# Step 8's rows by transposing transfer, a GpSimd drain put in order, and step 3's hidden values in two halves of columns

## Chip, core and metric

The kernel runs on one core of a Trainium2 chip: TensorE (PE), VectorE (DVE), ScalarE (ACT), GpSimd (POOL), SyncE (SP), which issues most transfers, and 16 DMA engines. The metric is the time of one execution in device microseconds, as the median of some runs. Profiles come from one execution that is profiled.

## What is computed

A feature-map attention over 8 batches, 8 heads and 576 positions of width 64, and behind it a mixture of 8 experts, of which each of the 4608 tokens takes one:

```python
x = attention(q, k, v, omega).reshape(4608, 512)
xn = x / (norm(x) + 1e-6); en = expert_emb / (norm(expert_emb) + 1e-6)
logits = xn @ en.T / tau
expert_idx = argmax(logits, axis=1)
gate_w = probs[arange(N), expert_idx]          # softmax of the logits
for e in range(8):
    mask = expert_idx == e
    h = maximum(x[mask] @ w1[e], 0.0)          # 512 -> 1024
    out[mask] = gate_w[mask, None] * (h @ w2[e])   # 1024 -> 512
```

All of it is float32. The kernel reaches that with float32r products: each operand is split into a rounded high part and what is left of it, and three products (high by high, high by low, low by high) are summed.

## The kernel before

**Two stages.** The first computes the attention in 36 tiles of 128 tokens and scatters each token's row from GpSimd into a table `xs` sorted by expert (L503). Two steps of the expert stage (steps 0 and 1, `first_steps`) are fitted into its last iterations; their outputs are the first two scatters to `y` (`store`, L270). The second stage is the loop over steps `t` = 2 to 37, in an order written out by hand for all engines (`manual_schedule`). A step is 128 rows of one expert.

**What a step does.** PE makes `pa` (rows by `w1`: two banks of 512 columns, 12 matmuls each) and `nu` (hidden values by `w2`: 24 matmuls), 48 in all. From step 6 on, the `nu` of a step belongs to the step two earlier, and step 5 has none. Rows and hidden values must be turned round (tokens to columns) before they can be used as PE's stationary operand. There are two ways:

- `turned` (L223): four PE transposes into a PSUM bank (`pt`), then ACT writes the high part (L227) and DVE the low part (L228).
- The transposing transfers: `apart16` (L924) splits 512 float32 columns into two planes of 16-bit words, one by DVE (L922, `moved`), one by ACT (L926). `turned16` (L929) has SP issue one transposing transfer for each plane (`t_<step>_0`, `t_<step>_1`, L933). When they have landed, `rejoin` (L941) puts the words together in `wd`: the hidden columns by DVE (L922), the row columns by ACT (L947). Then come `x_rounded` (L958, `xh`) and `x_left` (L962, `xl`) for the rows, and `summed` for the hidden values (L966 on ACT, `hh`, and L968 on DVE, `hl`).

The planes of step `t` take the hidden values of step `t` (1024 columns) and, where `far` holds, the rows of step `t + 2` (512 more). `XPE` = 9 is the first step whose rows go that way; rows of the steps before are turned on PE in the step ahead of their use. In steps 8 and 9 (`t in (XPE - 1, XPE)`) `xl` is made before the second `rejoin` of the hidden columns, in later steps behind it.

**What sets the order.** Each engine runs its own list in the order of the loop. SP issues, in this order within a step: a quarter of `w1`, a quarter of `w2`, the row block of step `t + 3` (`xload`, L158) and the two transposing transfers of step `t`. The planes have one buffer, so ACT's first `apart16` of a step waits until the transfers of the step before have read them. Row blocks live in a ring of six: the load of step 8's rows goes into the buffer of step 2's, and waits for step 2's scatter to `y`, which step 5 issues (`ended`, L1036) behind the scaling on DVE (L247). Every load of rows also waits for the one before it.

**Step 3's hidden values** are rejoined in step 4 (`early`): two rejoins of 1024 columns on DVE, `hh` of 1024 columns on ACT, `hl` of 1024 columns on DVE. Step 4's `nu` matmuls need both.

**The drain.** At `t == NPRE` (2) GpSimd gets a `drain` (L1020). Nothing ties it to its place. Other drains stand at every ninth step (L1051) and near the end (L1141).

Of the kernel before, what the change touches and what calls it, by code (L numbers as in the profile page):

```python
# [11 lines left out]
F32 = mybir.dt.float32  # L12
# [4 lines left out]
AF = mybir.ActivationFunctionType  # L17
ALU = mybir.AluOpType
# [6 lines left out]
E, F = 8, 1024  # L25
# [18 lines left out]
NSTAT = 38  # L44
WARM = 26
NSTEP = 64
XPE = 9
SHIFT = 5
BIGID = 1048576.0
EPS = 1e-6 * M  # L50
# [5 lines left out]
def attention_moe(ctx: ExitStack, tc: tile.TileContext, qT, kT, v1, omT, emb, tau, w1q, w2q, xs, out):  # L56
    nc = tc.nc
# [36 lines left out]
    first = const.tile([P, 1], F32, name="first")  # L94
# [8 lines left out]
    order = mybir.DependencyInfo(mybir.DependencyClass.NoSync, mybir.DependencyReason.DATA)  # L103
    put, got, outs, last_x, junks, early = [], [], [], [], [], []
# [173 lines left out]
    with ExitStack() as c1:  # L278
# [367 lines left out]
        mid, after, then, ends = {}, {}, {}, {}  # L646
# [207 lines left out]
    def sums(t, name, n):  # L854

        return [p2.tile([P, n], F32R, name=f"{name}{z}{t}", tag=f"{name}{z}", bufs=2) for z in "hl"]
# [6 lines left out]
    def halves(t, name, n):  # L863

        return placed.pop((name, t)) if (name, t) in placed else sums(t, name, n)
# [12 lines left out]
    def words(t):  # L878
        return p2.tile([P, F + DM], F32, name=f"wd{t}", tag="wd", bufs=1)
# [21 lines left out]
    xg, xt, hid, raws, po = {}, {}, {}, {}, {}  # L901
# [18 lines left out]
    def moved(to, src):  # L920

        nc.vector.tensor_reduce(to, src.unsqueeze(2), axis=AX.X, op=ALU.max)  # L922
# [14 lines left out]
    with tc.manual_schedule(engines={ET.PE, ET.Activation, ET.DVE, ET.Pool, ET.SP}):  # L937
        xt[NPRE] = pre_x[0]
        turn, ends = {}, NSTAT - 1

        def rejoin(u, wd, lo, hi, k):  # L941

            to, src = halved(wd)[:, lo:hi, k], turn[u][k][:, lo // P : hi // P].rearrange("p c r -> p (c r)")
            if lo < F:
                moved(to, src)
            else:
                nc.scalar.activation(to, src, AF.Copy)  # L947

        def joined(u):
            wd, n = words(u), turn[u][0].shape[1] * P  # L950
            assert n == F
            for k in range(2):
                rejoin(u, wd, 0, F, k)
            return wd, n
# [9 lines left out]
        def summed(u, wd):  # L964
            hid[u] = hh, hl = halves(u, "h", F)
            nc.scalar.activation(hh, wd[:, 0:F], AF.Relu)  # L966
            yield
            nc.vector.scalar_tensor_tensor(hl, wd[:, 0:F], 0.0, hh.bitcast(F32), op0=ALU.max, op1=ALU.subtract)  # L968
            yield
# [47 lines left out]
        for t in range(NPRE, NSTAT):  # L1017
            u = t - 1 if t < SHIFT else t - 2
            if t == NPRE:
                nc.gpsimd.drain()  # L1020
            far = XPE <= t + 2 < NSTAT
            near = t in (NPRE, ends)
            if t > NPRE + 1:
# [4 lines left out]
                weights("w2", t)  # L1028
            late = (t - 1) in turn
            early = late and (t < SHIFT or t == ends)  # L1030
            if early:
                sm = summed(t - 1, joined(t - 1)[0])
                next(sm)
                if t < ends:
                    next(sm)
            def ended():  # L1036

                for v in list(po):
                    scaled(po.pop(v), xg[v], gates[v])
                    store(v, xg[v])  # L1040
# [23 lines left out]
            computed("w1", t, products(pa[0], xt[t], "w1", par, low, 0, True, True))  # L1064
            if t == NPRE or NPRE + 1 < t < XPE - 1:
                xt[t + 1] = x_turned(t + 1, xg[t + 1])
            if near:
                h = words(t)
# [19 lines left out]
            if late and not early:  # L1088
                if wn[1] > F:
                    x_rounded(t - 1, wn[0])  # L1090
                    if t in (XPE - 1, XPE):
                        x_left(t - 1, wn[0])
# [6 lines left out]
            if late and not early:  # L1099
                sm = summed(t - 1, wn[0])  # L1100
                next(sm)
                if wn[1] > F and t not in (XPE - 1, XPE):
                    x_left(t - 1, wn[0])
# [48 lines left out]
    with tc.If(tot > NSTAT):  # L1152
        split("w1", ends)
        split("w2", ends)
        with tc.For_i(NSTAT, tot, 1) as i:
# [5 lines left out]
            h = hidden("x", x_turned("x", xgl), par)  # L1161
# [64 lines left out]
```

## Time and profile before

| | |
|---|---|
| median of 3 runs | 643.84 us (641.42 to 644.36) |
| profiled execution | 638.44 us, its span 636.9 us |
| PE, DVE, ACT, POOL busy | 620.7, 488.7, 414.3, 316.9 us |
| second stage on PE | from 232.4 us to the end |
| a step in its steady part | 10.88 us, 48 matmuls |

The page counts an engine as busy from an instruction's start to its end; matmuls overlap, and their starts are more exact than their ends. Times in the timeline are microseconds from the span's start. A bracket behind a row gives the idle time of the engine ahead of it, and who ended it. SPq is SP's queue of transfers: a row there is the issue, not the transfer itself. A row of windows gives the stretch, its length, then the busy time of PE, PEld, DVE, ACT and POOL with their instructions, TensorE's granted clock as a share of 2.4 GHz, the DMA engines' busy share and GB/s. In the chain of waits each piece is the work that the next one waited for.

### The profile page before, as it was taken

To read this page: it belongs to the slowest core of one execution; us is meant where nothing else is said; L and a number is where in the kernel's file an instruction comes from. 1 tells how busy PE (TensorE), PEld (TensorE's weight loads), DVE (VectorE), ACT (ScalarE), POOL (GpSimd) and SP (SyncE) were. 2 spreads that over 40 slices of the span, in tenths; PEclk is the share of its full clock that TensorE was granted. 3 is DMA by queue.
4 is the path that set the end of the run, shared out by engine and by line. 5 is a ranking of instruction groups with operands and counts; after the bars stand their busy time and mean duration, and the time that the engine had idled before them with its cause. 6 is when DMAs were issued, how large, how long until landed. Compare 5 with 4: busy or idle time off the path is not lost.

```text
span 636.9 us, 18610 instructions
## 1 busy us (share of the span) xinstructions
PE 620.7 (97%) x6339; PEld 531.2 (83%) x6340; DVE 488.7 (77%) x950; ACT 414.3 (65%) x1074; POOL 316.9 (50%) x404
## 2 busy tenths in 40 slices
PE   8999999999988999999999999999999999999996
PEld 7899999988877787788878888888888888888885
DVE  4799899899888736796788778788777778788652
ACT  6899899899977317654656565556565656565630
POOL 2014333337987434456365646464645555464623
PEclk9999999999999999999999999999999999999999
DMA  7547667678842278787988888888879897979741
GB/s 258 183 153 217 205 205 226 198 238 284 273 178 94 111 263 244 225 206 223 211 234 197 245 216 236 201 225 215 239 179 244 199 220 210 224 225 211 209 117 45
DMA packets 142362, 131.89 MB, mean 207 GB/s; under 512 B 106742, under 2 KB 106870, under 8 KB 142272
## 3 DMA queue, kind: packets, MB, share of 16 engines
q1 hardware_dynamic: 135808, 110.04, 65.4%
q0 software_dynamic: 6320, 20.38, 8.2%
q8 instruction: 57, 0.93, 0.6%
q10 hardware_dynamic: 144, 0.26, 0.2%
q14 instruction: 33, 0.27, 0.1%
HBM read 83.78 MB, written 21.97 MB: 166 GB/s over the span
## 4 chain that ended last, share of the span: by engine, by line
PE 72%; DVE 14%; ACT 6%; DMA 5%; issue 3%; POOL 0%; POOLq 0%; SPq 0%; DVEq 0%; ACTq 0%
PE pa L240 25%; PE nu L240 24%; PE pjk L328 5%; PE nub L424 4%; PE kva L354 4%; PE pjq L328 3%; DMA t<-pl 3%; DVE wd L922 3%; ACT ftk L339 2%; PE nub L400 2%; DVE nmq L332 2%; PE fs_o L240 2%; DVE pl L922 2%; PE fs_a L240 2%; ACT ftq L339 1%
## 5 line engine op out<-in xcount | busy, mean ns | idle before, releaser
L240 PE MATMUL nu<-w2h,hl 128*128 (+1 forms) x288 | 112.2, 390 | 0.5 <-DVE hl L968 0.5
L240 PE MATMUL nu<-w2h,hh 128*128 (+1 forms) x288 | 112.4, 390 | 0.0
L240 PE MATMUL nu<-w2l,hh 128*128 (+1 forms) x288 | 112.1, 389 | 0.0
L240 PE MATMUL pa<-w1h,xh 128*128 (+1 forms) x280 | 109.6, 391 | 0.1
L240 PE MATMUL pa<-w1h,xl 128*128 (+1 forms) x280 | 109.3, 390 | 0.3 <-DVE xl L962 0.3
L240 PE MATMUL pa<-w1l,xh 128*128 (+1 forms) x280 | 109.0, 389 | 0.0
L926 ACT ACTIVATE pl<-pa 128x512 uint16<-128x512 uint16 x68 | 39.9, 591 | 82.8 <-DMA t<-pl 59.7
L922 DVE TENSOR_REDUCE wd<-t 128x1024 uint16<-128x1024 uint16 x68 | 89.9, 1324 | 1.8 <-DMA t<-pl 1.8
L339 ACT ACTIVATE ftk<-pjk,nmk 128x128 f32<-128x128 f32 x288 | 85.4, 435 | 4.8 <-DVE nmk L332 4.6
L206 POOL TENSOR_TENSOR w1l<-raww,w1h 128x1024 f32 x33 | 80.2, 2431 | 10.1 <-DVE w1h L205 9.2
L339 ACT ACTIVATE ftq<-pjq,nmq 128x128 f32<-128x128 f32 x288 | 80.1, 433 | 7.6 <-DVE nmq L332 7.4
L922 DVE TENSOR_REDUCE pl<-pa 128x512 uint16<-128x512 uint16 x68 | 46.5, 686 | 46.2 <-ACT pl L926 45.7
L206 POOL TENSOR_TENSOR w2l<-raww,w2h 128x1024 f32 x33 | 79.5, 2408 | 3.8 <-DVE w2h L205 3.8
L328 PE MATMUL pjq<-om,qt 64*128 64x128 f32 x576 | 75.9, 283 | 1.5 <-ACT ftk L339 0.7
L966 ACT ACTIVATE hh<-wd 128x1024 fp32r<-128x1024 f32 x34 | 36.1, 1061 | 63.3 <-DVE wd L922 57.4
L328 PE MATMUL pjk<-om,kt 64*128 64x128 f32 x576 | 75.7, 283 | 0.3 <-DVE om L609 0.3
L328 PEld LDWEIGHTS pjk<-om,kt 64*128 64x128 f32 x576 | 64.4, 188 | 2.8 <-DVE om L609 0.5
L328 PEld LDWEIGHTS pjq<-om,qt 64*128 64x128 f32 x576 | 64.0, 188 | 2.3 <-ACT ftq L339 1.1
L240 PEld LDWEIGHTS nu<-w2h,hl 128*128 128x128 f32 x288 | 54.1, 188 | 12.1 <-DVE hl L968 0.9
L270 POOL DMA_INDIRECT y<-xgp x20 | 22.3, 1115 | 83.6 <-DVE xgp L247 75.0
L240 PEld LDWEIGHTS nu<-w2h,hh 128*128 128x128 f32 x288 | 54.0, 188 | 11.4 <-issue 0.2
L240 PEld LDWEIGHTS nu<-w2l,hh 128*128 128x128 f32 x288 | 54.1, 188 | 11.2
(311 smaller groups left out, 1258.9 us busy)
## 6 DMA issues: line engine op xcount, KB each, us to landing
raww<-w1q SPq DMA_DIRECT2D x38, 512.0 KB
raww<-w2q SPq DMA_DIRECT2D x38, 512.0 KB
qt<-qT SPq DMA_DIRECT2D x36, 256.0 KB
kt<-kT SPq DMA_DIRECT2D x35, 256.0 KB
xgp<-xs SPq DMA_DIRECT2D x20, 260.5 KB
xg<-xs SPq DMA_DIRECT2D x18, 260.5 KB
rf<-w1q SPq DMA_DIRECT2D x4, 512.0 KB
rf<-w2q SPq DMA_DIRECT2D x4, 512.0 KB
```

Of the source, the lines that this page charges most:

```text
L206: il = nc.gpsimd.tensor_tensor(at(l, dp), raw, at(h, dp).bitcast(F32), op=ALU.subtract)
L240: done.append(nc.tensor.matmul(dst, x[:, c * P : (c + 1) * P], ws.rearrange("p o f -> p (o f)"), start=(begin and i == 0 and k == 0), stop ...
L270: w = nc.gpsimd.indirect_dma_start(out=out, out_offset=bass.IndirectOffsetOnAxis(ap=xg[:, PAY - 1 : PAY].bitcast(I32), axis=0), in_=xg[:, ...
L328: nc.tensor.matmul(st["pj" + w, i, a][:, c, :], st[w, i][r, c, :], om[r, :], start=True, stop=True)
L332: nc.vector.tensor_reduce(nm, st["pj" + which, i, a], axis=AX.X, op=ALU.max, negate=True)
L339: nc.scalar.activation(ft[:, h, :], pj[:, h, :], AF.Exp, bias=nm[:, h : h + 1])
L354: nc.tensor.matmul(acc[c : c + 64, h, :], ft[:, h, c : c + 64], vt[:, 2 * h + a, :], start=begin and h == 0, stop=u == 4 + 4 * b and h == 3,)
L400: nc.tensor.transpose(nu[z][:, j * 64 : j * 64 + 64], st["fq", i, j // 4][r, j % 4, :], ident[r, r])
L424: nc.tensor.matmul(pn[a][z * 64 : z * 64 + 64, h, :], st["qp", i, z][:, 4 * a + h, :], kvs[sb, int(b)][:, h, a * HW : (a + 1) * HW], start ...
L922: nc.vector.tensor_reduce(to, src.unsqueeze(2), axis=AX.X, op=ALU.max)
L926: nc.scalar.activation(planes[1][:, o : o + 512], halved(src)[:, :, 1], AF.Copy)
L966: nc.scalar.activation(hh, wd[:, 0:F], AF.Relu)
```

## The change

Three edits. The first is one constant: `XPE` falls from 9 to 8. So step 8's rows ride along with step 6's hidden values (planes and transfers of 12 blocks of 128 columns and not 8), the four PE transposes of step 7 with their ACT and DVE work go, `rejoin`, `x_rounded` and `x_left` of rows come into step 7, and the steps in which `xl` is made early are 7 and 8 and no longer 8 and 9. The second ties the drain by an ordering without a wait to the last scatter to `y` so far. The profile of before has this drain at 2.4 us, ahead of the attention; the built program of after has it right behind the scatters of steps 0 and 1, ahead of step 0's split of `w2` on GpSimd. Nothing else on GpSimd changes its place. The third makes step 3's hidden values in two halves of columns: both rejoins and `hh` of one half, then of the other, then the two halves of `hl`.

```diff
-XPE = 9
+XPE = 8
...
             if t == NPRE:
-                nc.gpsimd.drain()
+                tc.add_manual_dep(nc.gpsimd.drain().ins, outs[-1].ins.name, order, reason="behind the first scatters")
...
-            if early:
+            if early and t < ends:
+                wd, hs = words(t - 1), halves(t - 1, "h", F)
+                hid[t - 1] = hs
+                parts = [slice(a * 512, (a + 1) * 512) for a in range(2)]
+                for c in parts:
+                    for k in range(2):
+                        rejoin(t - 1, wd, c.start, c.stop, k)
+                    nc.scalar.activation(hs[0][:, c], wd[:, c], AF.Relu)
+                for c in parts:
+                    nc.vector.scalar_tensor_tensor(hs[1][:, c], wd[:, c], 0.0, hs[0][:, c].bitcast(F32), op0=ALU.max, op1=ALU.subtract)
+            elif early:
                 sm = summed(t - 1, joined(t - 1)[0])
                 next(sm)
-                if t < ends:
-                    next(sm)
```

DVE in step 4, before: `wd` are the rejoined words, `t_3_0` and `t_3_1` the two transposed planes of step 3.

```order
L228 TENSOR_TENSOR xl_5616<-pt_5617,xh_5615 128x512
L922 TENSOR_REDUCE wd_5652<-t_3_0_5595 128x1024
L922 TENSOR_REDUCE wd_5652<-t_3_1_5597 128x1024
L968 SCALAR_TENSOR_TENSOR hl_5656<-wd_5652,hh_5655 128x1024
L145 TENSOR_LOAD tabi
```

The same place now:

```order
L228 TENSOR_TENSOR xl_5616<-pt_5617,xh_5615 128x512
L922 TENSOR_REDUCE wd_5652<-t_3_0_5595 128x512
L922 TENSOR_REDUCE wd_5652<-t_3_1_5597 128x512
L922 TENSOR_REDUCE wd_5652<-t_3_0_5595 128x512
L922 TENSOR_REDUCE wd_5652<-t_3_1_5597 128x512
L1040 SCALAR_TENSOR_TENSOR hl_5654<-wd_5652,hh_5653 128x512 x2
```

The rejoins come by halves of columns, each half with both planes, and `hl` has two instructions.

DVE in step 6, before: `pl_0` is DVE's plane, `t_5_0` and `t_5_1` the transposed planes of step 5.

```order
L922 TENSOR_REDUCE pl_0_5931<-pa_0_5933 128x512
L922 TENSOR_REDUCE wd_5970<-t_5_0_5899 128x1024
L922 TENSOR_REDUCE pl_0_5931<-pa_1_5934 128x512
L922 TENSOR_REDUCE wd_5970<-t_5_1_5901 128x1024
L968 SCALAR_TENSOR_TENSOR hl_5981<-wd_5970,hh_5980 128x1024
```

The same place now, where `xgp_103` holds the rows of step 8:

```order
L922 TENSOR_REDUCE pl_0_5935<-pa_0_5937 128x512
L922 TENSOR_REDUCE pl_0_5935<-xgp_103 128x512
L922 TENSOR_REDUCE wd_5976<-t_5_0_5903 128x1024
L922 TENSOR_REDUCE pl_0_5935<-pa_1_5938 128x512
L922 TENSOR_REDUCE wd_5976<-t_5_1_5905 128x1024
L968 SCALAR_TENSOR_TENSOR hl_5987<-wd_5976,hh_5986 128x1024
```

Step 8's rows have come in second place, ahead of the rejoin of step 5 and of the plane's second half, on which the transposing transfers of step 6 depend; ACT has the like for its plane.

ACT in step 7, before: `pt` is the bank of the PE transposes, `xg_5402` the rows of step 9, `pl_1` ACT's plane.

```order
L227 ACTIVATE xh_6052<-pt_6054 128x512
L926 ACTIVATE pl_1_6037<-pa_0_6038 128x512
L926 ACTIVATE pl_1_6037<-xg_5402 128x512
L926 ACTIVATE pl_1_6037<-pa_1_6039 128x512
L966 ACTIVATE hh_6087<-wd_6077 128x1024
```

The same place now:

```order
L926 ACTIVATE pl_1_6043<-pa_0_6044 128x512
L926 ACTIVATE pl_1_6043<-xg_5402 128x512
L947 ACTIVATE wd_6074<-t_6_0_5981 128x512
L947 ACTIVATE wd_6074<-t_6_1_5983 128x512
L926 ACTIVATE pl_1_6043<-pa_1_6045 128x512
L958 ACTIVATE xh_6085<-wd_6074 128x512
L966 ACTIVATE hh_6090<-wd_6074 128x1024
```

Step 8's `xh` has moved from the start of the step's row to its end, behind the planes and two rejoins that read step 6's transposed planes.

## Rows read from the trace of the kernel before

**Rows 1.** Windows, one a step (4, 7, 8, 11, 12): length, then busy by engine.
```profile
251.34:263.72 12.38, 11.87 (x53) 9.30 (x53) 9.08 (x11) 8.83 (x16) 6.11 (x3) 1.00 0.87 252
...
281.01:292.39 11.38, 11.38 (x54) 9.40 (x53) 8.73 (x15) 6.59 (x15) 6.16 (x4) 1.00 0.84 220
292.39:303.27 10.88, 10.88 (x50) 9.01 (x49) 7.58 (x12) 4.33 (x9) 5.95 (x3) 1.00 0.91 237
...
325.02:336.45 11.43, 11.18 (x49) 8.94 (x48) 8.62 (x13) 4.61 (x10) 6.03 (x4) 1.00 0.82 227
336.45:347.55 11.10, 11.10 (x50) 8.94 (x49) 8.76 (x12) 7.97 (x13) 5.95 (x3) 1.00 0.84 201
```

**Rows 2.** Timeline of PE at the end of step 4's first part.
```profile
257.70 0.40 PE L240 MATMUL nu<-w2l,hh 128*128 128x512 f32 x1
258.60 0.50 PE L240 MATMUL nu<-w2h,hl 128*128 128x512 f32 x1 [0.51 <-DVE hl L968]
```

**Rows 3.** The chain of waits, in order of time: start, length, what; steps 6 to 11.
```profile
269.83 0.61 ACT pl L926
...
281.45 5.22 DMA t<-pl
...
324.46 1.39 DVE xl L962
...
325.89 5.28 PE pa L240 x22
```

**Rows 4.** Timeline of DVE in step 4.
```profile
253.57 2.62 DVE L922 TENSOR_REDUCE wd<-t 128x1024 uint16<-128x1024 uint16 x2 [1.78 <-DMA t<-pl]
257.32 1.23 DVE L968 SCALAR_TENSOR_TENSOR hl<-wd,hh 128x1024 fp32r<-128x1024 f32 x1 [1.13 <-ACT hh L966]
```

**Rows 5.** Timeline of PE in step 7: the transposes.
```profile
283.73 0.60 PE L226 MATMUL pt<-ident,xgp 128*128 128x128 f32 x4
```

**Rows 6.** Timeline of SP's queue, steps 6 and 7.
```profile
276.70 0.33 SPq L158 DMA_DIRECT2D xgp<-xs  x1
...
279.71 0.33 SPq L158 DMA_DIRECT2D xg<-xs  x1
280.10 4.57 SPq L933 DMA_TRANSPOSE t<-pl  x2
...
292.08 0.33 SPq L158 DMA_DIRECT2D xg<-xs  x1
292.52 3.52 SPq L933 DMA_TRANSPOSE t<-pl  x2
```

**Rows 7.** What SP's queue waited for, 275 to 281 us: total, times, longest.
```profile
SPq L158 <- DMA y<-xgp: 2.6, 1, 2.6
SPq L158 <- DMA xgp<-xs: 0.9, 1, 0.9
```

**Rows 8.** Timeline of DVE, steps 6, 7 and 9.
```profile
278.91 0.67 DVE L922 TENSOR_REDUCE pl<-pa 128x512 uint16<-128x512 uint16 x1
...
289.74 0.66 DVE L922 TENSOR_REDUCE pl<-pa 128x512 uint16<-128x512 uint16 x1
...
313.12 0.76 DVE L962 TENSOR_TENSOR xl<-wd,xh 128x512 fp32r<-128x512 f32 x1
```

**Rows 9.** Timeline of ACT at the start of steps 7 and 8.
```profile
286.69 0.60 ACT L926 ACTIVATE pl<-pa 128x512 uint16<-128x512 uint16 x1 [1.14 <-DMA t<-pl]
...
298.49 0.60 ACT L926 ACTIVATE pl<-pa 128x512 uint16<-128x512 uint16 x1 [5.16 <-DMA t<-pl]
```

**Rows 10.** The drains by line: duration least, median, most (ns), first and last start.
```profile
L1020 POOLq DRAIN  x1: 406/406/406, 2.4 to 2.4; - x1
...
L1051 POOLq DRAIN  x3: 5648/5670/8961, 320.4 to 513.4; - x3
```

**Rows 11.** Timeline of POOL, steps 2 and 10.
```profile
243.01 4.77 POOL L203 TENSOR_TENSOR w2l<-raww,w2h 128x1024 fp32r<-128x1024 f32 x2 [7.08 <-ACT w2h L201]
...
322.88 2.40 POOL L206 TENSOR_TENSOR w2l<-raww,w2h 128x1024 f32 x1
```

## The prediction

> **What bounds the kernel now.** I read the windows step by step first. PE works without a gap in nearly all steps of the second stage: a step with 48 matmuls takes 10.88 us, so 0.227 us a matmul, and the granted clock stands at 1.00 of 2.4 GHz. Only where a step is longer can an edit gain anything [rows 1]. Step 4 has a wait for `hl`: the matmul that reads it starts 0.90 us behind the one before it, 0.67 more than the pitch [rows 2]. Step 7 is 0.50 longer than step 8, and the four transposes are what it has more [rows 1, 5]. Steps 11 and 12 are longer by 0.55 and 0.22. All other steps from 8 on take 10.88. So PE could win 0.67 + 0.50 + 0.55 + 0.22 = 1.94 us at most, 0.3% of the span.
>
> Then I read the chain of waits. From step 4 to step 6 it lies on PE. At 269.83 it leaves PE by the eviction of step 5's last bank and comes back only at 325.89, by `xl` of step 11 [rows 3]. Between these it runs in a loop: the transposing transfers land, ACT may write its plane, DVE evicts and rejoins, SP issues the next transfers. PE's wait in step 11 is this loop being late. So a gain on PE in steps 4 or 7 counts at the end only if the loop becomes earlier as well, and whatever makes the loop later counts in full. The rest of the working is about that loop.
>
> **Third edit, halves.** DVE's two rejoins run from 253.57 to 256.19; `hl` starts at 257.32 behind 1.13 of waiting for ACT [rows 4]. In halves the four rejoins take the same time, ACT's first `hh` fits under the last two, and half of `hl` (1.23 / 2) is ready at about 256.19 + 0.65 = 256.85, the rest one `hh` of half the columns and 0.6 later, at 257.5. PE wants the first half at 257.70 + 0.23 = 257.93 [rows 2] and the second 12 matmuls later. So the wait goes: -0.67, which moves PE in step 5 and with it the head of the loop. Next in line is `xl` of step 5, whose chain on DVE moves along.
>
> **Second edit, drain.** GpSimd is idle for 7.08 us ahead of 243.01, so from 235.93 on [rows 11], and the drain would start there. The drains in the trace last 0.41 to 8.96 us [rows 10], so this one ends between 236.3 and 244.9, and the split of `w2` behind it is late by 0 to 1.9. I take 0: two of the three drains of L1051 last 5.7, which is within the idle time. Below zero there is nothing, since PE waits for no work of GpSimd in these steps. What hides it is that idle time; its price without cover is a rival below.
>
> **First edit, what goes.** Four transposes on PE, 0.50 in step 7. ACT's and DVE's `turned` work of step 7 lies ahead of ACT's wait for the transfers of step 6, which ends at 286.69 [rows 9], and so frees nothing on the loop.
>
> **First edit, what comes.** In step 6 DVE and ACT must split the rows of step 8 in the middle of their planes. These rows are not there yet. Their load is issued at 276.70, held for 2.6 by step 2's scatter; the load behind it, at 279.71, waited for it to land [rows 6, 7]. So the rows land at about 279.65, 2.95 behind the issue. DVE is free for them at about 278.91 - 1.20 (the pitch of the rejoin ahead of that row) = 277.71 [rows 8]. It waits 1.94, works 0.60, and its second eviction moves from 278.91 to 281.45. With PE's 0.67 in hand at the head it is 280.8 and ends at 281.45; the transfers of step 6 are issued at 281.5 and not at 280.10, 1.4 later. ACT's split of the rows (0.6) goes on beside this.
>
> The transfers have 12 blocks now and not 8. From issue to ACT's release they took 6.59 with 8 blocks in step 6 (280.10 to 286.69) and 5.97 with 12 in step 7 (292.52 to 298.49) [rows 6, 9]. The lower bound is 5.97; the upper is 6.59 and half of the 4.57 that their issue took, 8.9. I take 6.6, nearest to both rows with a length, so ACT is released at 288.1, between 287.5 and 290.4, and not at 286.69.
>
> Step 7 then goes: release, 3.05 to DVE's second eviction (286.69 to 289.74), 0.66 for it [rows 8, 9]: the transfers of step 7 could be issued from 291.8 on. In the trace that was possible from 290.4 on, but SP stood until 292.08 in front of the load of step 10's rows, which waits for step 4's scatter, and issued them at 292.52 [rows 6]. So the loop has 1.7 of slack here, if that scatter is not late. It will be late by something: its scaling on DVE lies behind the rejoins of step 6, which have moved by 1.9. I take half, 0.9: the loop leaves step 7 by 0.9 later, with 0 and 1.9 as bounds.
>
> PE meanwhile: without waits step 8 begins at 292.39 - 0.67 - 0.50 = 291.22 and wants its `xl` two matmuls later, at 291.67. This `xl` comes 288.1 + 3.71 + 0.75 = 292.55, so PE waits 0.9. The hidden values of step 5 come 1.9 later too, at about 285; PE wants them at 286.3, so they are covered by 1.2.
>
> In step 9 `xl` (of step 10) moves behind one more rejoin, 1.3: from 313.12 to 314.4, done at 315.2, and 316.1 with the loop's 0.9 [rows 8]. Step 10 began at 303.27 + 10.88 = 314.15 and wants it at 314.6. So step 10 begins 1.5 later than before. After that PE is behind the loop: `xl` of step 11 at 325.85 + 0.9 = 326.75 is wanted at 325.47 + 1.5 = 326.97, and the waits of steps 11 and 12, 0.77, are gone.
>
> **Sum.** +1.5 - 0.77 = +0.73. On the profiled execution's 638.44 that is 639.2. The median of the three runs stands 5.4 above that execution, and I add the same 0.7 to it: 644.6. About 0.5%, 3.2 us, is what a measurement of this kernel can tell from no change, so the forecast is no difference.
>
> **Rivals.**
>
> The loop keeps up. If step 4's scatter lands no later than before, the loop leaves step 7 as it did: step 10 is then 0.6 late, 0.77 goes, -0.2 in all. If the loop's head carries its 0.67 through as well, it is -0.8, and with all waits gone -1.9. For it speaks the slack of 1.7, against it that DVE is later by 1.9 in step 6. About 643.4, from 641.9 to 643.7.
>
> GpSimd blocks DVE. `xl` of step 8 was computed out of PSUM; it will now read two operands in SBUF. Such an `xl` took 1.39 on the chain at 324.46, while GpSimd split `w2` from 322.88 to 325.28, and 0.76 at 313.12 [rows 3, 8, 11]. In step 7 GpSimd's two splits move by up to 1.9, to about where `xl` stands. If they meet, `xl`, the rejoin behind it and the rest of the loop are later by 0.6: 645.2. The Trainium skill has a rule on this (SBUF — State Buffer, Who interferes with whom): a DVE instruction with two SBUF inputs and a GpSimd instruction that reads SBUF exclude each other for a whole instruction. By that rule the trace agrees, with the 1.39 beside a GpSimd split.
>
> Slower: step 8's rows land late. They are the one new thing on which both ACT and DVE stand in step 6. The load waits for a scatter (2.6) and then takes 2.95 [rows 7]; each microsecond that either takes more moves the rejoins, the transfers of step 6 and, from 1.2 on, the hidden values for PE's step 7. From 2.5 on, so if the rows land behind 281.5 on this clock, the kernel is slower by over 0.5%; for 3 more it gives 644.6 + 3 = 647.6. Against it: the place of this load on SP's queue, and what stands ahead of it, have not changed.
>
> The drain holds GpSimd for 8.96 or more. The split of `w2` is then 1.9 late, with it the next weights and rows on SP's queue and, at worst, the transfers of step 3 by as much. `hl`'s first half comes at 258.75, and PE waits 0.8 where it waited 0.67. So edit three brings nothing and the loop starts 0.8 later than forecast: 645.4.
>
> The change does what it says, as the order of instructions shows; that the halves don't take PE's wait away is in the last rival.
>
> **Chances.** Forecast 0.46, loop keeps up 0.29, GpSimd blocks DVE 0.12, rows late 0.06, drain 0.05, anything else 0.02. Only late rows and part of the rest pass 0.5%: slower 0.05, faster 0.02, same 0.93. The range reaches from all PE waits gone (643.84 - 1.9 = 641.9) to the upper bound of the transfers of step 6, 2.3 more than taken (644.6 + 2.2 = 646.8).
>
> **What would show it.** In the profile after: step 4 at about 11.7 and no wait of PE for `hl`; a wait of DVE and ACT of 1 to 2 us for step 8's rows in step 6; ACT's release in step 7 near 288; PE waits for `xl` at the start of steps 8 and 10, and none in 11 and 12; a drain at about 236 that ends ahead of 243. I am wrong if steps 8 to 10 stay at 10.88 (the loop keeps up), if PE waits for hidden values in step 7 (rows late), or if the step 3 transfers are issued later than before (drain).

## The result and the profile after

The changed kernel takes 647.28 us (median of 22 runs), the kernel before 642.80 on the same chip (22 runs): a ratio of 1.0062, interval 1.0047 to 1.0078. That is 4.5 us more, just past the 0.5% that the prediction named as what can be told from no change; the forecast was +0.7. The runs of after also spread more, from 642.97 to 651.87, against 640.66 to 645.87: fourteen stand between 646.1 and 651.9, the other eight at or under 645.2.

The profiled execution of after is 647.85 (span 646.3) and stands 9.4 above the one of before (638.44). Not all of that is the change. The second stage begins at 236.44 on PE and not at 232.41, 4.0 later, but the execution of before that was profiled is faster than all 22 runs timed beside after. Whether the change makes the first stage longer is taken up with the experiments. From the start of the second stage to the start of step 14, behind which both kernels go at 10.88 a step, before takes 126.02 and after 131.33: +5.3. The windows of after (length, busy by engine, granted clock, DMA) for steps 2 with 3, 4, 7, 8, 9, 10 and 12 answer to [rows 1]:

```profile
236.44:258.14 21.70, 18.75 (x90) 14.88 (x88) 12.83 (x11) 13.25 (x21) 9.69 (x6) 1.00 0.82 278
258.14:271.30 13.16, 13.16 (x52) 10.59 (x53) 10.51 (x17) 8.73 (x18) 4.79 (x2) 0.87 0.77 232
...
288.61:299.49 10.88, 10.88 (x50) 9.01 (x48) 9.62 (x17) 7.32 (x16) 4.59 (x4) 1.00 0.90 252
299.49:312.17 12.68, 11.17 (x50) 8.93 (x48) 11.33 (x13) 5.07 (x9) 7.08 (x4) 1.00 0.69 187
312.17:323.72 11.55, 11.18 (x50) 8.94 (x49) 10.19 (x12) 7.20 (x12) 6.30 (x4) 1.00 0.78 211
323.72:334.78 11.06, 11.06 (x49) 8.93 (x48) 9.19 (x16) 7.76 (x18) 5.96 (x3) 1.00 0.85 218
...
345.66:356.89 11.23, 11.18 (x50) 8.94 (x48) 9.22 (x13) 8.32 (x14) 5.96 (x3) 1.00 0.84 213
```

Steps 2 and 3 took 18.93 before, so +2.77; step 4 +0.78; step 7 is 0.50 shorter, the four transposes; step 8 +1.80; step 9 +0.67; step 10 +0.18. Steps 11 to 13 together give 0.4 back. Two thirds of the loss stand in steps 2 to 4, where the forecast had a gain. The waits of PE in the second stage name what it waits for (total, times, longest):

```profile
PE pa L240 <- DVE w1l L203: 2.6, 1, 2.6
PE pa L240 <- DVE xl L962: 1.9, 2, 1.5
```

The first of them was no wait at all before. What stands behind it is the drain. By line (duration least, median, most in ns, first and last start), to be read against [rows 10]:

```profile
L1020 POOLq DRAIN  x1: 9688/9688/9688, 238.0 to 238.0; - x1
```

Such a row begins while GpSimd still works on what was queued ahead. Here that is a scatter until 239.92, so some 7.7 us are the drain's own, until 247.7; the last packets of the scatters end at 245.44 in the transfer records. The other three drains last 5.4 to 5.7 now, with two splits (4.8) inside, which leaves 0.6 to 0.8. GpSimd gets to its splits at 247.84, which is 11.40 behind the stage's start; it was 10.60 before [rows 11]. So the drain is 0.80 longer than its cover. GpSimd's timeline, then DVE's, in steps 2 and 3 of after:

```profile
247.84 4.75 POOL L203 TENSOR_TENSOR w2l<-raww,w2h 128x1024 fp32r<-128x1024 f32 x2 [7.91 <-ACT w2h L201]
254.54 2.37 POOL L203 TENSOR_TENSOR w2l<-raww,w2h 128x1024 fp32r<-128x1024 f32 x1 [1.96 <-ACT w2h L201]
```

```profile
250.32 3.35 DVE L203 TENSOR_TENSOR w1l<-raww,w1h 128x1024 fp32r<-128x1024 f32 x1 [2.64 <-ACT w1h L201]
...
254.79 3.20 DVE L203 TENSOR_TENSOR w1l<-raww,w1h 128x1024 fp32r<-128x1024 f32 x1
```

Before, the first of these `w1l` (of step 2) met a split as well, but later in that split's course, and took 2.28; the second (of step 3) was 0.77 ahead of GpSimd's third split. DVE, then GpSimd, of before:

```profile
246.57 2.28 DVE L203 TENSOR_TENSOR w1l<-raww,w1h 128x1024 fp32r<-128x1024 f32 x1 [2.93 <-ACT w1h L201]
...
249.98 1.21 DVE L203 TENSOR_TENSOR w1l<-raww,w1h 128x1024 fp32r<-128x1024 f32 x1
```

```profile
250.75 2.69 POOL L203 TENSOR_TENSOR w2l<-raww,w2h 128x1024 fp32r<-128x1024 f32 x1 [2.97 <-ACT w2h L201]
```

Now each of them begins 0.1 to 0.25 behind the start of a GpSimd split of 2.4 and ends 1.1 behind its end. Alone it takes 1.21, so DVE does next to nothing of it until GpSimd is done. PE, which needs `w1l` of step 3 for its next matmul, stands for 2.6 until 258.14. Then the granted clock falls (windows of 2 us; the clock is the third number from the right, behind it DMA's share and GB/s):

```profile
256.00:258.00 2.00, 0.00 (x0) 0.00 (x0) 2.00 (x2) 0.58 (x2) 0.91 (x1) 1.00 0.89 173
258.00:260.00 2.00, 1.86 (x7) 1.45 (x8) 1.75 (x3) 0.00 (x0) 0.00 (x0) 0.88 0.92 216
260.00:262.00 2.00, 2.00 (x6) 1.52 (x6) 2.00 (x4) 1.16 (x2) 0.00 (x0) 0.50 0.99 360
262.00:264.00 2.00, 2.00 (x10) 1.64 (x9) 1.01 (x3) 1.97 (x4) 0.00 (x0) 0.76 1.00 346
```

0.50 is 1.2 GHz, the lower level. Between 259.79 and 262.35 six matmuls follow one another in 0.43 each and not in 0.227, so 1.2 us go there; with the four transposes behind them step 4 is 1.6 longer than in the same kernel without the drain's move (13.16 and 11.57, below). This eats what the halves win in step 4.

In step 6 the rows of step 8 came late, as forecast. DVE, SP's queue and ACT, steps 6 and 7 of after:

```profile
287.18 0.69 DVE L922 TENSOR_REDUCE pl<-xgp 128x512 uint16<-128x512 uint16 x1 [1.81 <-DMA xgp<-xs]
```

```profile
289.69 3.30 SPq L933 DMA_TRANSPOSE t<-pl  x2
```

```profile
295.31 0.60 ACT L926 ACTIVATE pl<-pa 128x512 uint16<-128x512 uint16 x1 [0.18 <-DMA t<-pl]
```

And the two early `xl`, of steps 8 and 9, each beside a GpSimd split of `w2` (298.63 and 310.15):

```profile
298.96 2.60 DVE L962 TENSOR_TENSOR xl<-wd,xh 128x512 fp32r<-128x512 f32 x1
...
310.59 2.50 DVE L962 TENSOR_TENSOR xl<-wd,xh 128x512 fp32r<-128x512 f32 x1
```

The chain of waits of after (start, length, what) shows all four places in order: a `w1l`, the late rows, two `xl`. Before, it ran on PE from step 4 to step 6 [rows 3].

```profile
254.87 3.13 DVE w1l L203
258.14 4.42 PE pa L240 x12
...
284.30 2.79 DMA xgp<-xs
...
299.03 2.52 DVE xl L962
...
310.66 2.43 DVE xl L962
```

### The profile page after: what moved, and what is told of

It reads as the page before. It is cut to its first block, busy times and chain, and to the rows that moved or that the text cites. A ratio compares the mean times of both kernels' runs of the same rounds, so it can differ in the third digit from the quotient of the medians.

```text
span 646.3 us, 18612 instructions
## 1 busy us (share of the span) xinstructions
PE 623.0 (96%) x6335; PEld 532.6 (82%) x6336; DVE 495.7 (77%) x954; ACT 416.3 (64%) x1078; POOL 316.2 (49%) x404
## 4 chain that ended last, share of the span: by engine, by line
PE 74%; DVE 12%; ACT 5%; DMA 4%; issue 3%; POOL 0%; POOLq 0%; SPq 0%; DVEq 0%; ACTq 0%
PE pa L240 25%; PE nu L240 23%; PE pjk L328 6%; PE kva L354 5%; PE nub L424 5%; PE pjq L328 4%; PE nub L400 3%; DVE wd L922 2%; DMA t<-pl 2%; DVE pl L922 2%; PE fs_o L240 2%; ACT ftq L339 1%; ACT ftk L339 1%; PE fs_a L240 1%; DVE xl L962 1%
## 5 line engine op out<-in xcount | busy, mean ns | idle before, releaser
L922 DVE TENSOR_REDUCE wd<-t 128x1024 uint16<-128x1024 uint16 (+1 forms) x70 | 89.9, 1289 | 0.3 <-DMA t<-pl 0.2
L240 PEld LDWEIGHTS pa<-w1h,xl 128*128 128x128 f32 x280 | 52.8, 189 | 14.7 <-DVE xl L962 3.5
L240 PEld LDWEIGHTS pa<-w1h,xh 128*128 128x128 f32 x280 | 52.8, 189 | 13.7 <-issue 3.0
L270 POOL DMA_INDIRECT y<-xg x18 | 21.3, 1181 | 86.8 <-DVE xg L247 86.5
## 6 DMA issues: line engine op xcount, KB each, us to landing
qt<-qT SPq DMA_DIRECT2D x36, 256.0 KB
kt<-kT SPq DMA_DIRECT2D x35, 256.0 KB
```

The lines of the kernel that those rows point to most:

```text
L240: done.append(nc.tensor.matmul(dst, x[:, c * P : (c + 1) * P], ws.rearrange("p o f -> p (o f)"), start=(begin and i == 0 and k == 0), stop ...
L270: w = nc.gpsimd.indirect_dma_start(out=out, out_offset=bass.IndirectOffsetOnAxis(ap=xg[:, PAY - 1 : PAY].bitcast(I32), axis=0), in_=xg[:, ...
```

## The experiments

The three parts alone and the change without the drain ran on one chip (before: 639.10, 35 runs), the next four on a second (638.92, 31 runs), the last four on a third (642.70, 35 runs). "To 14" is the time from the second stage's start to step 14's start in the profiled execution; before it is 126.02.

| kernel | ratio | interval | stage starts | steps 2, 3 | step 4 | step 8 | to 14 |
|---|---|---|---|---|---|---|---|
| after | 1.0062 | 1.0047 to 1.0078 | 236.44 | 21.70 | 13.16 | 12.68 | 131.33 |
| drain alone | 1.0023 | 1.0006 to 1.0040 | 234.18 | 19.64 | 12.16 | 10.88 | 126.45 |
| transfers alone | 1.0038 | 1.0021 to 1.0055 | 231.98 | 18.91 | 12.16 | 12.60 | 127.62 |
| halves alone | 1.0002 | 0.9984 to 1.0020 | 232.70 | 18.92 | 11.58 | 10.88 | 126.75 |
| after without the drain's move | 1.0023 | 1.0009 to 1.0037 | 232.25 | 18.91 | 11.57 | 12.76 | 127.89 |
| no first drain | 0.9989 | 0.9975 to 1.0003 | 232.51 | 18.93 | 12.17 | 10.88 | 126.03 |
| after and the drain at the start | 1.0077 | 1.0052 to 1.0103 | 232.31 | 21.50 | 13.11 | 12.68 | 131.31 |
| drain behind the third split | 1.0015 | 0.9998 to 1.0031 | 233.42 | 18.93 | 11.56 | 12.35 | 128.43 |
| transfers, `xl` apart from GpSimd | 1.0028 | 1.0015 to 1.0041 | 231.29 | 19.20 | 11.89 | 11.40 | 128.20 |
| after, `w2l` behind `w1l` | 1.0025 | 1.0012 to 1.0038 | 235.62 | 19.79 | 11.37 | 12.75 | 129.26 |
| transfers, rows at hand | 1.0013 | 0.9997 to 1.0029 | 234.85 | 19.13 | 11.93 | 11.38 | 127.96 |
| both cures on the transfers | 1.0011 | 0.9993 to 1.0029 | 236.89 | 18.92 | 12.22 | 11.40 | 126.56 |
| halves, no first drain | 0.9991 | 0.9970 to 1.0013 | 236.90 | 18.92 | 11.57 | 10.88 | 125.09 |

**The drain alone.**

```diff
             if t == NPRE:
-                nc.gpsimd.drain()
+                tc.add_manual_dep(nc.gpsimd.drain().ins, outs[-1].ins.name, order, ...)
```

> Before with the ordered drain alone. Theory: the drain (9.69 us in the changed kernel, from 238.0 to 247.69) holds GpSimd's first splits of w2, the next one then falls onto DVE's split of w1 (3.20 us and not 1.21), and PE waits 2.6 us at the head of step 4 and runs at half its clock for 3 us behind that. Then steps 2 and 3 are longer by 2.5 to 3 and step 4 by 1 to 2, and the time is 3 to 4.5 us over before, near the whole of the change's +4.5. Rival: the profiled execution of the changed kernel was 4 us longer in the attention stage too, so its second stage is no measure either; the drain has cover and the time is that of before within 1 us.

It costs 1.5 us by the ratio and 2.4 by the two medians, less than the 3 to 4.5 of the theory. The drain is 10.09 long, from 235.3; GpSimd's splits begin 11.33 behind the stage's start. In this execution the first `w1l` met a split and the second did not:

```profile
248.20 3.15 DVE L203 TENSOR_TENSOR w1l<-raww,w1h 128x1024 fp32r<-128x1024 f32 x1 [2.78 <-ACT w1h L201]
...
252.47 1.21 DVE L203 TENSOR_TENSOR w1l<-raww,w1h 128x1024 fp32r<-128x1024 f32 x1
```

PE waited 0.8 for `w1l` here and not 2.6. So the drain is not free by itself, and what it costs depends on which of the two engines begins first, by tenths of a microsecond.

**The transposing transfers alone.**

```diff
-XPE = 9
+XPE = 8
```

> Before with XPE = 8 alone. Theory: xl of steps 8 and 9 now meets GpSimd's split of w2 (2.60 and 2.50 us in the changed kernel), PE waits for it at the head of steps 8 and 9, step 7 loses 0.50, steps 11 and 12 lose their waits: +1 to +2 us in all. Rival (the prediction's own): the loop of transfers is late by 0.9 and xl meets nothing, +0.7; or the meeting is a matter of timing which the drain set up, then xl takes 0.7 and the time is -0.5 to +0.5.

It costs 2.4 us by the ratio and 2.3 by the medians; the drain's interval overlaps with this one, so the runs don't tell which part is dearer. Step 8 and step 9 pay:

```profile
291.30:303.90 12.60, 11.27 (x49) 9.05 (x49) 11.33 (x14) 5.07 (x9) 7.00 (x4) 1.00 0.71 191
303.90:315.48 11.58, 11.21 (x49) 8.93 (x48) 10.45 (x12) 7.56 (x12) 6.34 (x4) 1.00 0.77 206
```

DVE waits 1.82 for the rows in step 6, the two `xl` take 1.90 and 2.59, and PE waits 1.7 for them in all:

```profile
291.39 1.90 DVE L962 TENSOR_TENSOR xl<-wd,xh 128x512 fp32r<-128x512 f32 x1
...
302.24 2.59 DVE L962 TENSOR_TENSOR xl<-wd,xh 128x512 fp32r<-128x512 f32 x1
```

Two causes offer themselves here, the late rows and the meetings of `xl` with GpSimd; the later runs take them apart.

**The halves alone.**

```diff
-            if early:
+            if early and t < ends:
...
+                for c in parts:
+                    for k in range(2):
+                        rejoin(t - 1, wd, c.start, c.stop, k)
+                    nc.scalar.activation(hs[0][:, c], wd[:, c], AF.Relu)
```

> Before with step 3's hidden values in halves alone. Theory: step 4 is 0.67 us shorter, and the loop's head with it, so the time is 0.3 to 0.7 us below before. Rival: the loop gives nothing on, steps 11 and 12 wait longer, and the time is that of before within 0.2.

The wait of step 4 goes, 11.58 and not 12.38, and the time stays. Windows of steps 4, 10 and 11:

```profile
251.62:263.20 11.58, 11.58 (x52) 9.44 (x53) 8.39 (x14) 8.12 (x17) 5.34 (x3) 1.00 0.85 256
...
314.00:325.32 11.32, 11.20 (x49) 8.98 (x49) 10.06 (x18) 7.31 (x17) 5.18 (x3) 1.00 0.81 209
325.32:337.28 11.96, 11.20 (x49) 8.93 (x48) 8.88 (x12) 5.06 (x9) 6.53 (x4) 1.00 0.81 216
```

PE is 0.8 earlier, but steps 9 to 12 are 1.5 longer in all than in before (11.22, 11.32, 11.96, 11.29), so step 14 begins 0.73 later. The loop of transposing transfers is what is late, though not at its head: the transfers of step 6 are issued 0.8 earlier than in before, counted from the stage's start, and then take 8.48 to ACT's release and not 6.59. SP's queue, then ACT:

```profile
279.60 4.87 SPq L933 DMA_TRANSPOSE t<-pl  x2
```

```profile
288.08 0.60 ACT L926 ACTIVATE pl<-pa 128x512 uint16<-128x512 uint16 x1 [3.02 <-DMA t<-pl]
```

This is one execution. The last run below has the same edit, its transfers of step 6 take 6.65, and the gain of step 4 stays. So it isn't shown that the loop must give the gain back.

**After, without the drain's move.**

```diff
-                tc.add_manual_dep(nc.gpsimd.drain().ins, outs[-1].ins.name, order, ...)
+                nc.gpsimd.drain()
```

> The changed kernel with the drain as in before (unordered, so at the start). Theory: the drain carries most of the loss, so this is 0 to 2 us over before, and 3 to 4 below the changed kernel. Rival: the step 8 rows carry it, then this is as slow as the changed kernel, 4 us over before. If the attention stage's length hangs on the drain at the start, this and the xpe and halves kernels begin the second stage near 232.4 us, and the drain kernel near 236.4.

The ratio falls from 1.0062 to 1.0023, and the two intervals are apart, so the drain is worth 0.39% in the whole change, 2.5 us. Alone it was 0.23%, with an interval too wide to tell the two apart; the three parts alone add up to 0.63%, about the whole. Steps 2 to 4 are as with the halves alone (18.91 and 11.57), step 8 has the price of the transfers:

```profile
290.88:303.64 12.76, 11.18 (x49) 8.93 (x48) 10.53 (x13) 5.06 (x9) 7.16 (x4) 1.00 0.71 187
```

**No first drain.** In the first executions the second stage had begun at 232.0 to 232.7 with the drain at the start, and at 234.18 and 236.44 where it had been moved. So a theory was that the drain at 2.4 us keeps the first stage on time.

```diff
-            if t == NPRE:
-                nc.gpsimd.drain()
```

> The kernel before without the first GpSimd drain at all, neither at 2.4 us nor behind the scatters (it stood at 2.4 us and took 0.41). Theory 'the drain at the start keeps the first stage on time': the second stage began on PE at 232.41 (before), 231.98, 232.70 and 232.25 (three kernels with the drain at 2.4 us), and at 234.18 and 236.44 in the two where it had been moved. So without it the second stage begins at 234 to 236.5, steps 2 and 3 stay at 18.9 (no drain behind the scatters), and the time is 1.5 to 4 us longer, a ratio of 1.002 to 1.006. Rival 'the moved drain costs only where it stands, and the start of the second stage scatters from run to run': begins at 232 to 233, ratio 1.000 +- 0.001.

The theory falls: the stage begins at 232.51 and the time is no longer than before.

**After, and the drain at the start as well.**

```diff
             if t == NPRE:
+                nc.gpsimd.drain()
                 tc.add_manual_dep(nc.gpsimd.drain().ins, outs[-1].ins.name, order, ...)
```

> The kernel after with the drain at the start kept as well as the one behind the scatters. Theory 'the start drain counts': the second stage begins at 232.0 to 232.7 and not at 236.44; the drain behind the scatters is still 9 to 10 us, w1l of step 3 still meets the GpSimd split (3.2 us and not 1.21), steps 2 and 3 take 20 to 22, and of the +4.5 only the second stage's own loss is left: ratio 1.003 to 1.0045. Rival 'the drain behind the scatters is what costs, in either stage': nothing is won, ratio 1.006, second stage begins at 234 to 236.5.

Nothing is won, 1.0077, although the stage begins at 232.31. Its second stage repeats that of after, 131.31 to step 14, and both `w1l` meet a split:

```profile
246.28 3.12 DVE L203 TENSOR_TENSOR w1l<-raww,w1h 128x1024 fp32r<-128x1024 f32 x1 [2.74 <-ACT w1h L201]
...
250.52 3.14 DVE L203 TENSOR_TENSOR w1l<-raww,w1h 128x1024 fp32r<-128x1024 f32 x1
```

So what the drain costs in this execution stands behind its new place. On the third chip the last three kernels of the table, in which the drain stands at 2.4 us or nowhere, begin the stage at 234.85 to 236.90, where before itself is slower by 3.6 by the medians. So a start at 236 comes about without the drain's move, and the 4.0 between the two profiles ahead of the second stage is most likely the chip's. It stays an inference, since before was not profiled on that chip.

**The drain behind GpSimd's third split.**

```diff
-            if t == NPRE:
-                tc.add_manual_dep(nc.gpsimd.drain().ins, outs[-1].ins.name, order, ...)
...
                 split("w2", u)
+                tc.add_manual_dep(nc.gpsimd.drain().ins, outs[-1].ins.name, order, ...)
                 down(u, high)
```

> The kernel after, with the ordered drain moved behind the split of step 2's second weights (GpSimd's third split, ended at 256.9 in the kernel after; in the kernel before GpSimd is idle there for 6.3 us ahead of 259.71). Theory 'the 9.7 us are a wait for the last scatters to land': the drain is then 0.3 to 1 us long, no split is late, w1l of step 3 takes 1.21 again, steps 2 and 3 take 18.9, step 4 about 11.6; what is left is the first stage's late start (0 to 4) and the 1.9 of the transposing transfers: ratio 1.003 to 1.006 if the start drain counts, 1.002 to 1.003 if not. Rival 'the drain has work of its own for each transfer issued before it': it takes 9 to 10 us here too, GpSimd's split of step 4's first weights is 3.5 us late (263 and not 259.7 on the clock of before), step 4 or 5 waits for it and is 1 to 3 longer.

Both lengths that were expected are wrong:

```profile
L1124 POOLq DRAIN  x1: 6316/6316/6316, 251.8 to 251.8; - x1
```

GpSimd's third split (251.80, 2.66 long) lies inside this row, so 3.6 are the drain's own, in a row that begins some 16 us behind the last scatter: neither a mere wait for landing nor the whole length again. It fits into GpSimd's idle time ahead of the next split (6.30), no split is late, and `w1l` of step 3 takes 1.21 again:

```profile
250.99 1.21 DVE L203 TENSOR_TENSOR w1l<-raww,w1h 128x1024 fp32r<-128x1024 f32 x1
```

Steps 2 to 4 are as without the drain's move, and so is the time within the intervals (1.0015 and 1.0023). On the same chip the drain right behind the scatters gave 1.0077, with an interval apart from this one: its place decides (that kernel has the drain at the start besides, which costs nothing, as the run without a first drain shows). An ordered drain costs nothing that can be told where its cover is real.

**After, with GpSimd's third split behind DVE's `w1l` of step 3.** This leaves the drain long and takes away one meeting.

```diff
+        if (wn, t) == ("w2", NPRE):
+            tc.add_manual_dep(il.ins, spl["w1", NPRE + 1][1].ins.name, sync, ...)
```

> The kernel after with one dependency more: GpSimd's split of step 2's second weights waits until DVE has made w1l of step 3, so that these two don't stand side by side (in the kernel after they did: 3.20 us for w1l and not 1.21, a wait of PE of 2.6, then about 3 us at half the granted clock). The drain stays behind the scatters and long. Theory 'the meeting of DVE's w1l and GpSimd's split is how the drain costs': w1l of step 3 takes 1.2, PE's wait at the head of step 3 falls from 2.6 to 0.3 to 0.8, the granted clock stays at 1.00 there, steps 2 and 3 take 19.2 to 19.9 and not 21.7, the spread of the runs falls, ratio 1.002 to 1.004 (what the transposing transfers cost is left). Rival 'GpSimd's lateness itself costs': the wait of PE moves to a later weight or row, step 4 or 5 is longer by what was won, ratio 1.005 to 1.007.

The ratio is 1.0025, about what after has without the drain's move. The drain is longer than ever, 10.32, and GpSimd as late. DVE and GpSimd:

```profile
249.47 1.22 DVE L203 TENSOR_TENSOR w1l<-raww,w1h 128x1024 fp32r<-128x1024 f32 x1 [2.62 <-ACT w1h L201]
...
252.55 1.46 DVE L203 TENSOR_TENSOR w1l<-raww,w1h 128x1024 fp32r<-128x1024 f32 x1 [0.65 <-ACT w1h L201]
```

```profile
247.18 5.75 POOL L203 TENSOR_TENSOR w2l<-raww,w2h 128x1024 fp32r<-128x1024 f32 x2 [8.55 <-ACT w2h L201]
254.81 2.40 POOL L203 TENSOR_TENSOR w2l<-raww,w2h 128x1024 fp32r<-128x1024 f32 x1 [1.89 <-ACT w2h L201]
```

Steps 2 and 3 take 19.79, step 4 takes 11.37, and the granted clock stays at 1.00. In this execution it was the first meeting that went the other way: DVE began first, its `w1l` took 1.22, and GpSimd stood (5.75 for two splits and not 4.75), so that the new dependency had nothing left to do. That it works fits the runs: of after's 22, 14 are above 646.0 us, of these 12 none, the highest 645.85, with before at 642.8 and 642.7. It would fit that the meeting does not happen in the other eight of after's runs either; no profile shows one of them. So lateness of GpSimd costs little; its meeting with DVE's `w1l` costs.

The Trainium skill has the rule for this (SBUF — State Buffer, Who interferes with whom): a DVE instruction with two SBUF inputs and a GpSimd instruction that reads SBUF exclude each other for a whole instruction, and the order of issue decides which one stands. The trace agrees in both directions: 3.20 to 3.35 for `w1l` in after where GpSimd was first, and one more microsecond for GpSimd here where DVE was first.

**The transfers, with `xl` apart from GpSimd's split.**

```diff
                     if t in (XPE - 1, XPE):
                         x_left(t - 1, wn[0])
+                        tc.add_manual_dep(spl["w2", u][1].ins, left[-1].ins.name, sync, ...)
```

> The transposing transfers alone (the kernel before with step 8's rows turned by transfers), and the GpSimd split of the second weights in steps 7 and 8 made to wait for DVE's xl there, so that the two don't stand side by side. In the kernel with the transfers alone xl of steps 8 and 9 took 1.90 and 2.59 and PE waited 1.7 for them, ratio 1.0038. Theory 'the meeting of xl and the GpSimd split is what costs': both xl take 0.7, PE's wait for them in steps 8 and 9 goes or is under 0.3, step 8 takes 10.9 to 11.3 and not 12.60, step 9 10.9 to 11.2 and not 11.58; 1.2 to 1.7 us less, ratio 1.0010 to 1.0020. Rival 'the loop of transposing transfers is late by itself': xl is short but begins later or the wait only moves to steps 10 to 12; step 14 begins as late as before and the ratio stays at 1.003 to 1.004.

Both `xl` take 0.68 and 0.69 now, and the price stays, 1.0028 against 1.0038. The wait moves from step 8 to steps 9 and 10:

```profile
302.27:314.29 12.02, 11.04 (x49) 8.85 (x48) 7.39 (x10) 6.64 (x11) 8.36 (x4) 1.00 0.86 211
314.29:326.85 12.56, 11.27 (x49) 9.05 (x50) 11.87 (x19) 8.98 (x19) 5.95 (x3) 1.00 0.81 207
```

The loop is what is late, and a faster `xl` only shows it one step later. The meeting that decides in steps 2 and 3 does not decide here by itself.

**The transfers, with rows at hand.** Step 8 is computed on step 7's rows, so that no load is waited for in step 6.

```diff
-                apart16(xg[t + 2][:, 0:DM], planes, F)
+                apart16(xg[t + 1 if t == XPE - 2 else t + 2][:, 0:DM], planes, F)
```

> The transposing transfers alone (step 8's rows turned by transfers), but step 8 is computed on the rows of step 7, which landed one step earlier, so that step 6's splits of the rows wait for no load; the load of step 8's rows stays. Theory 'the rows are late, and the loop of transposing transfers carries that on': DVE's wait for rows in step 6 (1.82) goes, the transfers of step 6 are issued 1 to 1.4 us earlier, as in the kernel before, and the waits of PE in steps 8 and 9 (1.7 in all) shrink to under 0.6; ratio 1.000 to 1.002. Rival 'it is the meeting of xl with the GpSimd split': xl of steps 8 and 9 stays at 1.9 to 2.6, ratio 1.003 to 1.004. Third: the fifth instruction more per step on DVE (rejoin, xl) is enough by itself to make the loop longer than PE's 10.88 from step 7 on; then both waits go and the ratio is still 1.002 to 1.004, the waits in steps 9 to 11.

The ratio falls to 1.0013, 1.6 us less than with the transfers alone by the point values (the intervals overlap), though `xl` of step 9 still meets a split and takes 2.67. DVE no longer waits for rows, and the transfers are issued 16.47 behind step 5's start, as in before (16.38). But they land later:

```profile
282.38 5.67 SPq L933 DMA_TRANSPOSE t<-pl  x2
```

```profile
291.72 0.60 ACT L926 ACTIVATE pl<-pa 128x512 uint16<-128x512 uint16 x1 [3.89 <-DMA t<-pl]
```

From issue to ACT's release 9.34, where it was 5.62 in after and 6.34 with the transfers alone, and 6.59 with 8 blocks in before [rows 6, 9]. That costs step 7 what the earlier issue brings (12.06), and in this execution step 14 begins no earlier than with the transfers alone (127.96 and 127.62). What makes them slow here was not tried.

**Both cures.**

```diff
+                apart16(xg[t + 1 if t == XPE - 2 else t + 2][:, 0:DM], planes, F)
...
+                        tc.add_manual_dep(spl["w2", u][1].ins, left[-1].ins.name, sync, ...)
```

> Both cures on the transposing transfers alone: step 8 computed on step 7's rows, so that nothing waits for the load in step 6, and GpSimd's split of the second weights in steps 7 and 8 behind DVE's xl. If late rows and the meeting of xl and split are together the whole price: steps 7 to 10 take 10.9 to 11.1 each, ratio 0.999 to 1.001 (the four transposes, 0.50, are won). Rival 'the loop is longer than PE's step by itself': PE waits 1 to 2 us in all in steps 8 to 12 still, ratio 1.002 to 1.003.

1.0011, no better than rows alone by the runs. Steps 9 and 12:

```profile
308.34:319.22 10.88, 10.88 (x49) 9.01 (x48) 8.44 (x11) 7.31 (x12) 7.69 (x4) 1.00 0.83 220
...
340.98:352.57 11.59, 11.17 (x49) 8.93 (x48) 9.40 (x13) 8.17 (x14) 5.96 (x3) 1.00 0.84 223
```

Steps 9 to 11 are free of waits, and one of 0.7 comes back in step 12. In the profiled executions the two cures do more together than each alone: the transfers of step 10 are issued 91.5 behind the stage's start in before, 93.3 to 93.5 with the transfers alone and with either cure, and 92.3 with both. So late rows and the meeting with GpSimd each keep the loop late, one execution of each kernel says. Even so the 0.50 of the transposes is not won; the transfers of step 6 take 8.9 to ACT's release here too.

**Halves without a first drain.** A version that might have beaten both.

```diff
-            if t == NPRE:
-                nc.gpsimd.drain()
...
+            if early and t < ends:
```

> A kernel that could beat both: the one before without its first GpSimd drain (0.9989 [0.9975, 1.0003] alone) and with step 3's hidden values in two halves (1.0002 alone). Theory 'PE's gain in step 4 is given back by the loop of transposing transfers': step 4 takes 11.6, steps 9 to 12 wait by 0.3 to 1 more than in the kernel before, ratio 0.998 to 1.001. Rival 'the gain lasts': steps 8 to 12 stay as before and the ratio is 0.997 to 0.998.

0.9991, interval 0.9970 to 1.0013: faster than after, not to be told from before. In the profiled execution the stage to step 14 is 0.9 shorter than before: step 4 keeps its gain, and steps 11 and 12 wait about as before (11.30 and 11.12), which is the rival's picture and not the theory's, though the ratio can't part the two. No kernel here beats before by more than the measurement can tell.

## Why the prediction was off

**The drain** is the step that failed, and it made most of the difference. The prediction took its price as zero, with 5.7 us of drain under 7.08 of idle time. The reading of [rows 10] was wrong to begin with: both the 5.7 and the 8.96 hold two splits that GpSimd was still working on, and the drains' own parts were 0.8 and 4.1 (the two splits behind 320.50 ended at 325.28, the drain at 329.4). No row of before showed a drain right behind some 40 scatters that are still on their way; it measured 7.7 of its own (7.6 to 8.4 in the three other kernels that have it there). The lateness was then under the rival's (0.8 against 1.9), but its price was not. "PE waits for no work of GpSimd in these steps" was true and beside the point: PE waits for DVE's `w1l`, and DVE stands while GpSimd reads. Before already showed what such a meeting does to `w1l` (2.28 in step 2, 1.21 in step 3). The rival priced the late drain at 0.8 by `hl`, the measurement gives 2.5 by the ratios (1.0062 without 1.0023), and 2.77 and 0.78 in steps 2 to 4 of the profiled execution, with the half clock behind a wait of 2.6 as a term that had no place in the sum.

**GpSimd blocks DVE** was a rival of 0.12 at 645.2, for `xl` of step 8. The mechanism was right and was looked for at one place of three. `xl` took 2.60 and 2.50, where the working had 0.75 for a free one and 1.39 for one beside a split; at that place taking the meeting away alone gains nothing that can be told, as the run with `xl` apart shows. Where it counted, `w1l` in steps 2 and 3, the two instructions began 0.77 apart in before.

**The rows of step 8** went as worked out. DVE's wait was put at 1.94 and is 1.81. From issue to ACT's release 6.6 was taken and 5.62 measured, just under the lower bound of 5.97. PE's wait for `xl` in step 8 was put at 0.9 and is 1.5 in after, 1.3 with the transfers alone, most of it the meeting: there `xl` began 0.09 behind the step's start (291.39 and 291.30), so at its free length of 0.68 it would have left some 0.3. So the 0.9 came near by luck: the lateness was smaller, and the meeting made up for it.

**What the loop makes of it** was mis-sized. The change without the drain's move is the forecast's other two edits. In its profile step 10 begins 1.23 later than before, counted from the stage's start (forecast +1.5), but the -0.77 behind it did not come: steps 11 and 12 take 11.63 and 11.20 and so wait 0.3 more than before, and step 10 is 0.33 longer. That makes +1.87 at step 14 where the sum had +0.73. The working held the loop 0.9 behind up to `xl` of step 11. The issue of the transfers is 0.8 behind in step 7, as taken, but 2.4 in step 8 and 1.9 in step 10. By the runs this part (1.0023, interval 1.0009 to 1.0037, so 0.6 to 2.4 us) can't be told from the forecast; the drain's part can.

**The halves** did what was said: no wait for `hl` in step 4. In after this can't be seen in the step's length, because the half clock takes it back. Whether the gain lasts to the end stays open (lost in one profiled execution, kept in another; 1.0002 alone).

**The signs named beforehand**: step 4 at 11.7 came only without the drain's move (11.57), the wait for the rows came, ACT's release in step 7 came 6.70 behind the step's start (forecast 7.1, from 288.1 and before's 281.01), PE's waits for `xl` came in steps 8 and 9 and not at 10, with a small one in 12 (11.23), and the drain ended 0.8 behind its cover.

**The range.** It ended at 646.8, 3.0 above the 643.84 of the shown median; the result is 4.5 above its own comparison. The range had the transfers' upper bound in it (called 2.3 there, and added as 2.2) and no bound for a drain with transfers still in flight, which no row showed.

## What to carry to other kernels

A move on an idle engine is free only if nothing behind it shifts against another engine with which it shares something. Ask of each instruction that becomes later what runs on the neighbour at that moment, and how far apart the two stand: here 0.8 us of lateness cost 2.5. A row that begins on a queue may hold work of the engine that stood ahead: take that off before it is used as a length.

In a loop that is about as long as PE's step, a cheaper step, a shorter `xl` or a won wait can return as a wait one to three steps on, as it did in most of these profiles. Look at when each round of the loop issues its transfers, and how long these take, before a gain on PE is counted.

## What the runs showed of the hardware

- A GpSimd drain ahead of all scatters took 0.40 to 0.41 us, in the whole row. Without the engine's own work in front, it took 0.6 to 0.8 at most of the later places, 3.6 in a row that began some 16 us behind the first stage's last scatter (4.1 at 320.4 in before, where it is the first one behind these scatters as well; 0.6 at that place in the kernels that had one before it), and 7.6 to 8.4 right behind them.
- After PE had stood for 2.6 us and had been at work again for 1.4, the granted clock fell to 0.50 for 3.4 us; 256.0 to 258.0 with PE idle still shows 1.00. In the kernel with both drains it fell likewise, behind a wait of 2.5. With a wait of 0.8 (the drain alone), and of 1.5 in step 8, it stayed at 1.00.
- Transposing transfers of 12 blocks took between 5.6 and 9.3 us from issue to release at one and the same step, in kernels that issued them up to 1.9 apart, counted from step 5's start; those of 8 blocks took 6.6 to 8.5 there.
